# Attention mix on one core: width of the V products, queues of the Q and K moves, and the planner's numbers around them

## The chip, the cores and the metric

The kernel runs on one core of a Trainium2 chip. The metric is the device time of one execution in microseconds; each kernel is timed in several runs and the median counts. Engines are named as in the profile: PE (TensorE matmul) with PEld (its weight loads), ACT (ScalarE), DVE (VectorE), POOL (GpSimd) and SP (SyncE). SP and POOL matter here as queues too: each starts DMA transfers in the order of its own program, and a transfer that has to wait holds everything behind it on that queue.

## The reference

Two attention layers read the same input `x` (2048 rows of 512) and are mixed by a gate per row. Layer A has 32 heads of 16 columns that share one K and one V; layer B has a K and a V for each head.

```
g = sigmoid((x * gate_w).sum(-1, keepdims=True))
# A: q = x @ wq (32 heads of 16), k = x @ wk (16), v = x @ wv (16)
# B: q, k, v = x @ wqkv (32 heads of 16 each)
p = softmax(q @ k.T * 16 ** -0.5)      # per head, 2048 x 2048
o = p @ v
a = o_heads_joined @ wo
return g * a + (1 - g) * b
```

There are 64 heads in all, so 64 x 2048 x 2048 exponentials. Scores and probabilities stay on the core.

## The kernel before, in words

The heads are worked in 8 groups of eight (A and B in turn), each group for two halves of the query rows, each half for two sets of four heads: 32 phases. A phase has 32 *quads*, and a quad is two score tiles of 128x1024. So there are 2048 score tiles. Each is made by 8 matmuls of 512 columns on PE (names `sc`, line L564), which run side by side on tiles of 64x32 of the array, into one of two PSUM buffers. ACT takes the exponential of the tile into a buffer `prob` (L571). Some of the tiles go another way: PE writes them into the spare PSUM buffer, and DVE works out the exponential as a chain of 7 operations, one conversion (L751), two masks (L754, L758) and four steps of a polynomial (L763), into buffers `vec`. Both kinds are then multiplied with V on PE (L612) and summed in PSUM.

PSUM has two further buffers, `pair[0]` and `pair[1]`. One sums the V products of the phase; the other, the *spare*, is used by everything else in turn: projections of Q, K and V (24 products of 512 columns each, L188, from `project`), the turning of V (`turned`), the output projections (`o_unit`), and the score tiles for DVE. Each of these fills the spare on PE, and DVE then has to empty it before the next may begin. DVE and PE each work strictly in the order of their program.

A projection of Q or K is emptied by DVE as a high and a low fp16 part, `hi` and `lo` (L394, L397), and `lay` then moves 16-row pieces of them into the layout that the scores read: 32 DMAs for each projection. All of them are issued by POOL (L352). When a phase's sums are complete, DVE copies them to `raw` (L665), SP issues 10 moves of them into `dT` (the sums of the probabilities) and `oT` (L505, from `normalised`), and DVE takes the reciprocal (L511) and multiplies. Weights come one after another (`load_w`): SP loads one, POOL splits it into a high and a low half (L204 to L206), SP makes a copy with the partition halves swapped (`swapped`, L193), and DVE takes an absolute maximum of it (L197) for a check of the input's range.

The order of all this isn't written out by hand. The program is generated by a planner (`_Plan`, `pe_step`) that carries a clock of its own for each engine, charges each job a fixed price, and gives PE the next job that fits. `limit` is the time by which the next score tile has to begin: the later of the time at which it can (`t`) and `SLACK` ns behind the start of the last exponential. `value_job` offers a V product in pieces, 256 columns for tiles from ACT and 128 columns for tiles from DVE, where 256 columns are priced at `HALF` = 430 ns. `spare_job` decides between a projection and a tile for DVE: if no unit is in a hurry (its due time less than `SPARE` ns away), it is a tile for DVE. `ISSUE` is the price of a move, `LANDS` the time until it has landed. If a price is wrong, the order stays as it was planned, and an engine waits.

## Time and profile before

| | |
|---|---|
| Median of 3 runs | 2022.6 us (2015.66 to 2030.31) |
| Profiled execution, its own time | 2003.99 us |
| Its span | 2001.7 us |
| Mean granted clock of PE | 0.98 |
| ACT busy | 1816.2 us, 91% of the span |
| PE busy | 1840.3 us, 92% |
| DVE busy | 1198.4 us, 60% |
| POOL busy | 542.4 us, 27% |
| Exponentials on ACT / score tiles on DVE | 1946 / 102 |

The profile is of one execution. Busy time of a PE that pipelines its matmuls isn't a measure of its peak, so the table alone doesn't tell which engine sets the time; for that, one looks at what the idle time of each engine waits for. A row of the timeline gives start and length in us, engine, line, operation, and in brackets the idle time just before and what ended it. A row of the waits gives the total in us, how often, and the longest.

### The profile page before, as it was taken

What the parts mean: (1) busy time and instruction counts of PE and PEld (TensorE: products, weight loads), DVE (VectorE), ACT (ScalarE), POOL (GpSimd) and SP (SyncE); (2) the same over time, 40 slices, a digit from 0 to 9 for tenths busy, and PEclk for the clock granted to TensorE, in tenths of its full rate; (3) what the DMA queues carried; (4) which work ended last, traced back from release to release, by engine and by line L of the source; (5) the groups of instructions that cost most, each with busy time, mean ns of one, the idle gap of its engine ahead of it and who ended that gap; (6) DMA issues with size and microseconds to landing.
All of it is one profiled execution on the core that took longest, in us unless ns stands there. A gap on an engine that the chain in (4) does not pass through costs nothing.

```text
span 2001.7 us, 130978 instructions
## 1 busy us (share of the span) xinstructions
PE 1840.3 (92%) x61680; PEld 1155.0 (58%) x61680; DVE 1198.4 (60%) x1352; ACT 1816.2 (91%) x1961; POOL 542.4 (27%) x891
## 2 busy tenths in 40 slices
PE   8999998998999998998999999899799999898995
PEld 5566564555565665655666566555466565555552
DVE  5166521968385734578457752687657775158983
ACT  4899996998999998998999999899799999998994
POOL 4314303451042503325013430353203233034000
PEclk9999999999999999999999999999999999999997
DMA  5222212223132232133224241141402314116011
GB/s 140 47 34 47 68 36 72 46 56 62 30 62 44 50 56 51 37 62 66 47 40 79 43 70 20 40 87 42 76 5 49 64 38 76 32 27 162 15 57 56
DMA packets 140435, 109.73 MB, mean 55 GB/s; under 512 B 86432, under 2 KB 94880, under 8 KB 139888
## 3 DMA queue, kind: packets, MB, share of 16 engines
q0 software_dynamic: 37376, 50.35, 14.6%
q1 hardware_dynamic: 100560, 48.27, 10.2%
q8 instruction: 485, 7.95, 1.6%
q10 hardware_dynamic: 1952, 2.66, 0.4%
q14 instruction: 62, 0.51, 0.1%
HBM read 14.75 MB, written 33.55 MB: 24 GB/s over the span
## 4 chain that ended last, share of the span: by engine, by line
PE 47%; ACT 31%; issue 9%; DVE 6%; POOL 4%; DMA 2%; SPq 1%; ACTq 0%; DVEq 0%; POOLq 0%
ACT prob L571 31%; PE pair L612 23%; PE sc L564 13%; PE pair L188 8%; DVE vec L763 2%; POOL Qa L352 2%; DVE sum L471 1%; DVE vec L751 1%; SPq L505 1%; PE pair L564 1%; POOL K L352 1%; PE pt L265 1%; DMA wqb<-in_B_wqkv_dram 1%; DVE raw L665 0%; DMA oT<-raw 0%
## 5 line engine op out<-in xcount | busy, mean ns | idle before, releaser
L571 ACT ACTIVATE prob<-sc 128x1024 f32<-128x1024 f32 x1946 | 1805.6, 1093 | 128.3 <-PE sc L564 124.4
L612 PE MATMUL pair<-prob,vA 64*32 64x256 f32 x15680 | 695.8, 378 | 16.9 <-issue 15.7
L612 PE MATMUL pair<-prob,vB 64*32 64x256 f32 x15456 | 657.7, 381 | 11.6 <-issue 10.6
L564 PE MATMUL sc<-Qa,kA 64*32 64x512 f16 x7840 | 477.9, 383 | 18.3 <-issue 6.3
L564 PE MATMUL sc<-Qb,K 64*32 64x512 f16 x7728 | 442.6, 388 | 25.7 <-issue 4.2
L612 PEld LDWEIGHTS pair<-prob,vA 64*32 64x32 f32 x15680 | 350.3, 105 | 81.2 <-issue 38.8
L763 DVE SCALAR_TENSOR_TENSOR vec<-vec,vec 128x1024 f32<-128x1024 f32 x306 | 373.3, 1236 | 2.4
L564 PEld LDWEIGHTS <-K 64*32 64x32 f16 x8192 | 209.0, 91 | 282.5 <-issue 210.9
L612 PEld LDWEIGHTS pair<-prob,vB 64*32 64x32 f32 x15456 | 329.5, 106 | 71.4 <-issue 29.2
L564 PEld LDWEIGHTS <-kA 64*32 64x32 f16 x8192 | 213.3, 90 | 212.2 <-issue 157.1
L352 POOL DMA_DIRECT2D K<-hikb x128 | 65.7, 518 | 385.3 <-DVE hikb L394 382.7
L751 DVE TENSOR_SCALAR vec<-pair 128x1024 int32<-128x1024 f32 x102 | 124.1, 1217 | 71.9 <-PE pair L564 71.2
L352 POOL DMA_DIRECT2D Qa<-hiqa x115 | 59.6, 518 | 360.6 <-DVE hiqa L394 348.8
L763 DVE SCALAR_TENSOR_TENSOR vec<-vec 128x1024 f32<-128x1024 f32 x102 | 125.1, 1226 | 1.0
L481 POOL DMA_DIRECT2D out_dram<-sum x48 | 59.7, 1243 | 239.2 <-DVE sum L471 215.3
L511 DVE RECIPROCAL dT<-dT 128x256 f32<-128x256 f32 (+1 forms) x66 | 111.0, 1690 | 18.8 <-DMA dT<-raw 18.8
L352 POOL DMA_DIRECT2D Qb<-hiqb x128 | 66.2, 517 | 200.1 <-DVE hiqb L394 197.8
L471 DVE TENSOR_SCALAR sum<-pair,gate_up 128x512 f32<-128x512 f32 x112 | 78.5, 740 | 50.9 <-PE pair L188 50.7
L665 DVE COPY raw<-pair 128x1024 f32<-128x1024 f32 x32 | 39.1, 1222 | 116.7 <-PE pair L612 116.5
L188 PE MATMUL pair<-w16ob,o 64*32 64x512 f16 x1536 | 92.1, 396 | 15.3 <-ACT o L517 7.0
L188 PE MATMUL pair<-xT,w16kb 64*32 64x512 f16 x1536 | 101.6, 376 | 4.7 <-issue 4.6
L188 PEld LDWEIGHTS <-o 64*32 64x32 f16 x3072 | 60.7, 94 | 64.4 <-issue 27.4
(137 smaller groups left out, 1564.1 us busy)
## 6 DMA issues: line engine op xcount, KB each, us to landing
out_dram<-sum POOLq DMA_DIRECT2D x48, 512.0 KB, 5.9
dT<-raw SPq DMA_DIRECT2D x126, 64.0 KB, 2.7
vB<-vB SPq DMA_DIRECT2D x32, 128.0 KB, 5.1
Qb<-hiqb POOLq DMA_DIRECT2D x128, 32.0 KB, 2.3
Qb<-loqb POOLq DMA_DIRECT2D x128, 32.0 KB, 2.2
K<-hikb POOLq DMA_DIRECT2D x128, 32.0 KB, 2.3
K<-lokb POOLq DMA_DIRECT2D x128, 32.0 KB, 2.3
out_dram<-sum SPq DMA_DIRECT2D x8, 512.0 KB, 4.3
```

Of the source, the lines that this page charges most:

```text
L188: nc.tensor.matmul(outs[n : n + COLS, i], lhs[i][rows(i), n : n + COLS], rhs[i][rows(i)], start=start, stop=stop)
L265: nc.tensor.matmul(pt[rows(i), 2 * c + w, :], x_tiles[k][:, i, at : at + ROWS], ident, start=c % 2 == w == 0, stop=c % 2 == w == 1)
L352: fns.append(lambda q=queues[(8 * p + n) % len(queues)], dst=dst, src=hilo[part][at]: q.dma_start(dst, src))
L471: nc.vector.tensor_scalar(state["sum"][:, e], pair[1][:, e], g, None, op0=ALU.mult)
L481: plan.on_pool([lambda: nc.gpsimd.dma_start(dst, state["sum"], accum_op=ALU.add)], t, 1500)
L511: nc.vector.reciprocal(d[:, c : c + cut], d[:, c : c + cut])
L564: nc.tensor.matmul(bank[a : a + COLS, hh], k[rows(hh), key : key + COLS], Q[src, gi, half, p][rows(hh), j * BLK : (j + 1) * BLK], start=Tr ...
L571: nc.scalar.activation(probs[u], sc, AF.Exp, scale=SCALE / (UP * UP))
L612: nc.tensor.matmul(pair[0][32 * k : 32 * k + 32, i, cols], v[rows(i)], probs[2 * m + k // 2][rows(i), hh, cols], start=first, stop=last)
L665: nc.vector.tensor_copy(state["raw"], full)
L751: nc.vector.tensor_scalar(tile("p").bitcast(I32), pair[1], SCALE / (UP * UP) / math.log(2) * 2.0 ** 23, None, op0=ALU.mult)
L763: nc.vector.scalar_tensor_tensor(p, m if i == 3 else p, VEC[i], m if i else w, op0=ALU.add, op1=ALU.mult)
```

## The change

V products are offered in one piece of 512 columns where the planner's room up to `limit` is at least 860 ns and the product hasn't been begun, else in pieces of 256, for tiles of both kinds. `SLACK` is 404 instead of 400. The moves of Q and K alternate between SP and POOL, with a clock for SP in the planner. The swapped copies of the weights are issued by POOL instead of SP. V's swapped copy is one transfer for each partition half instead of two. The rest are numbers and conditions of the planner: the price of a turn, the times of the buffers `sum`, a lower `SPARE`, 3000 ns of margin before a tile of the next phase is given to DVE, a bound `LATE` on jobs between the two tiles of a quad, and 30000 instead of 15000 ns for the reading of the output before the last group.

```diff
-SLACK = 400
+SLACK = 404
 TO_VEC, FROM_VEC, CHAINED = 255, 150, 130
-ISSUE, LANDS = 520, 3200
+ISSUE, ISSUE_SP, LANDS, SUM_LANDS = 480, 600, 3200, 6500
...
+    def on_sp(self, fns, ready, ns):
+
+        for fn in fns:
+            fn()
+            self.sp = max(self.sp, ready) + ns
+        return self.sp
...
         def halve():
             split_weight(pair[0][:, 0], pair[0][:, 1], w)
-            swapped(pair[1], pair[0], nc.sync)
+            swapped(pair[1], pair[0], nc.gpsimd)
...
-            at = plan.on_pool([halve], t, 3300)
+            at = plan.on_pool([halve], t, 4800)
...
         def put(hilo, t):
-            queue = (nc.gpsimd,)
             to = q_tiles(src, gi, half) if part == "q" else k_tiles(gi, half)
             parts = (0, 1, 0, 1) if part == "q" else (0, 0, 1, 1)
             for p in range(4):
-                done = plan.on_pool(lay(hilo, to[p], p, parts, queue), t, ISSUE)
+                fns = lay(hilo, to[p], p, parts, (nc.sync, nc.gpsimd))
+                done = max(plan.on_sp(fns[0::2], t, ISSUE_SP), plan.on_pool(fns[1::2], t, ISSUE))
                 ready[part, src, gi, half, p] = done + LANDS
...
-                swapped(vB[1][:, ts, :, 0], vB[0][:, ts, :, 0], nc.sync)
-                swapped(vB[1][:, ts, :, 2], vB[0][:, ts, :, 2], nc.sync)
+                done = plan.on_sp([lambda: swapped(vB[1][:, ts], vB[0][:, ts], nc.sync)], end, 2 * ISSUE_SP)
                 free["spare"] = end + FROM_VEC
                 free["hilo"] = end
-                ready["v", gi, half] = end + LANDS + 1000
+                ready["v", gi, half] = done + LANDS + 1000
...
-        jobs = [(lambda t=t, part=part: job(t, part), 155) for t in range(8) for part in range(2)]
+        jobs = [(lambda t=t, part=part: job(t, part), 60) for t in range(8) for part in range(2)]
...
-                    plan.on_pool([lambda: nc.gpsimd.dma_start(dst, state["sum"], accum_op=ALU.add)], t, 1500)
+                    done = plan.on_pool([lambda: nc.gpsimd.dma_start(dst, state["sum"], accum_op=ALU.add)], t, 1300)
+                sum_free[state["turn"]] = done + SUM_LANDS
...
+            begin = end + TO_VEC
+            if n + 1 < len(groups):
+                state["turn"] = turn[0]
+                turn[0] ^= 1
+                begin = max(begin, sum_free[state["turn"]])
             for e in range(2):
-                plan.vec(lambda e=e: take(e), 620, 1, end + TO_VEC, (), then if e else None)
+                plan.vec(lambda e=e: take(e), 660, 1, begin, (), then if e else None)
...
+        plan.sp = max(plan.sp, now) + len(moves) * ISSUE_SP
...
-    def value_job(now, mine):
+    def value_job(now, mine, room):
...
-        wide = BLK // (2 if mine else 4)
+        wide = BLK if n == 0 and room >= 2 * HALF else BLK // 2
         ns = HALF * wide * 2 // BLK
 
         def job():
-            values(m, slice(n * wide, (n + 1) * wide))
-            going[mine] = m, n + 1
-            if (n + 1) * wide == BLK:
+            values(m, slice(n, n + wide))
+            going[mine] = m, n + wide
+            if n + wide == BLK:
...
-            if max(laid(ph, NT - 1, phases[ph][2] + e) for e in range(2)) > now:
+            if max(laid(ph, NT - 1, phases[ph][2] + e) for e in range(2)) + 3000 > now:
...
-    JOB, AFTER, SPARE, WORK, EXTRA = 900, 3000, 20000, 1500, 7000
+    JOB, AFTER, SPARE, WORK, EXTRA, LATE = 900, 3000, 10000, 1500, 7000, 400
...
-        mine, other = (lambda: value_job(now, True)), (lambda: value_job(now, False))
+        mine, other = (lambda: value_job(now, True, limit - now)), (lambda: value_job(now, False, limit - now))
...
-            if job and now + job[1] <= limit:
+            if job and now + job[1] <= (limit if get is mine or not part[0] else min(limit, t + LATE)):
...
-        ready["late"] = plan.pe + 15000
+        ready["late"] = plan.pe + 30000
```

Since the planner sets the order, the change moves instructions all through the program. Counted over the whole order, ACT has 1926 exponentials instead of 1946 and DVE 122 tiles instead of 102. PE's V products (L612, now L624) stand in 12,624 matmuls instead of 17,200: 15,568 of 256 columns and 1,632 of 128 before, 3,760 of 512 and 8,864 of 256 now. Lines of the changed kernel are 7 to 12 higher. Three places follow.

The first is on PE, in the middle of the first group of layer A, where the second half of the keys of layer B's first group is projected (`w16kb00` is that weight; `pair` is a PSUM buffer; `sc276` is score tile 276). Before:

```order
L564 LDWEIGHTS K00_5601
L564 MATMUL sc276_7749<-Qb000_4410,K00_5601 32x512
L612 MATMUL pair1_83<-prob0_97,vB0_91 32x256 x4
L612 MATMUL pair1_83<-prob1_98,vB0_91 32x256 x4
L188 LDWEIGHTS w16kb00_737
L188 MATMUL pair0_82<-xT_84,w16kb00_737 32x512
```

Now the same projection begins here:

```order
L576 LDWEIGHTS kA_88
L576 MATMUL sc229_6473<-Qa013_2027,kA_88 32x512
L624 MATMUL pair0_82<-prob0_97,vA1_90 32x256 x4
L624 MATMUL pair0_82<-prob1_98,vA1_90 32x256 x4
L195 LDWEIGHTS w16kb00_737
L195 MATMUL pair1_83<-xT_84,w16kb00_737 32x512
```

The projection has moved from behind score tile 276 to behind score tile 229. Tile 288 is the first that reads this second half of the keys.

The second place is SP's queue, where the weights of the second group of layer B are loaded (`wkb1`, `wvb1`, `wqb1`; `w16...` are their halves; `raw5` and `oT102` belong to the normalisation of phase 5). Before:

```order
L505 DMA oT102_10671<-raw5_10669 32x512
L505 DMA oT102_10671<-raw5_10669 16x512
L193 DMA w16kb11_10574<-w16kb10_10573 64x1024 x2
L219 DMA wvb1_10843<-in_B_wqkv_dram 128x4x128
L193 DMA w16vb11_10846<-w16vb10_10845 64x1024 x2
L219 DMA wqb1_11011<-in_B_wqkv_dram 128x4x128
L193 DMA w16qb11_11014<-w16qb10_11013 64x1024 x2
```

Now:

```order
L516 DMA oT102_9975<-raw5_9973 32x512
L516 DMA oT102_9975<-raw5_9973 16x512
L359 DMA Qa100_10038<-hiqa10_10008 16x1024 x4
L359 DMA Qa101_10039<-hiqa10_10008 16x1024 x4
L359 DMA Qa102_10040<-hiqa10_10008 16x1024 x4
L359 DMA Qa103_10041<-hiqa10_10008 16x1024 x4
L226 DMA wvb1_10116<-in_B_wqkv_dram 128x4x128
L226 DMA wqb1_10241<-in_B_wqkv_dram 128x4x128
```

The copies of the halves have gone from this queue, and half of the moves of a Q projection stand ahead of the two loads.

The third place is DVE at the same time of the program (`stats` are the maxima, `sum0` takes an output projection out of the spare buffer, `vec` belongs to the chains). Before:

```order
L197 TENSOR_REDUCE stats_87<-w16kb10_10573 128x1
L763 SCALAR_TENSOR_TENSOR vec1_104<-vec1_104,vec5_108 128x1024
L197 TENSOR_REDUCE stats_87<-w16vb10_10845 128x1
L763 SCALAR_TENSOR_TENSOR vec1_104<-vec1_104,vec6_109 128x1024
L197 TENSOR_REDUCE stats_87<-w16qb10_11013 128x1
L471 TENSOR_SCALAR sum0_110<-pair1_83,gate_up_96 128x512 x2
```

Now:

```order
L204 TENSOR_REDUCE stats_87<-w16kb10_9877 128x1
L775 SCALAR_TENSOR_TENSOR vec6_109<-vec0_103 128x1024
L204 TENSOR_REDUCE stats_87<-w16vb10_10118 128x1
L476 TENSOR_SCALAR sum0_110<-pair0_82,gate_up_96 128x512 x2
L775 SCALAR_TENSOR_TENSOR vec6_109<-vec6_109,vec0_103 128x1024
L204 TENSOR_REDUCE stats_87<-w16qb10_10243 128x1
L775 SCALAR_TENSOR_TENSOR vec6_109<-vec6_109,vec0_103 128x1024
```

The emptying of the spare into `sum0` now stands ahead of the maximum of `w16qb`, and one operation of a chain lies between the maxima of `w16kb` and `w16vb` as before.

11 lines of the change are left out of this document (5 added, 6 removed).

## The prediction, made before the changed kernel was run

> **What bounds the kernel now.** I read the page first, then ACT's timeline, then what PE waited for, then each large gap on the engines around it.
>
> ```profile
> span 2001.7 us, 130978 instructions
> PE 1840.3 (92%) x61680; PEld 1155.0 (58%) x61680; DVE 1198.4 (60%) x1352; ACT 1816.2 (91%) x1961; POOL 542.4 (27%) x891
> PE 47%; ACT 31%; issue 9%; DVE 6%; POOL 4%; DMA 2%; SPq 1%; ACTq 0%; DVEq 0%; POOLq 0%
> L571 ACT ACTIVATE prob<-sc 128x1024 f32<-128x1024 f32 x1946 | 1805.6, 1093 | 128.3 <-PE sc L564 124.4
> ```
>
> PE and ACT look equally full, and the chain runs through both. ACT's timeline decides; these are a run without a gap and the gaps that the sum below uses:
>
> ```profile
> 176.74 81.81 ACT L571 ACTIVATE prob<-sc 128x1024 f32<-128x1024 f32 x89 [0.66 <-PE sc L564]
> ...
> 321.54 1.02 ACT L571 ACTIVATE prob<-sc 128x1024 f32<-128x1024 f32 x1 [14.86 <-PE sc L564]
> 324.99 65.30 ACT L571 ACTIVATE prob<-sc 128x1024 f32<-128x1024 f32 x71 [2.42 <-PE sc L564]
> ...
> 448.68 1.02 ACT L571 ACTIVATE prob<-sc 128x1024 f32<-128x1024 f32 x1 [2.19 <-PE sc L564]
> ...
> 457.64 1.03 ACT L571 ACTIVATE prob<-sc 128x1024 f32<-128x1024 f32 x1 [3.65 <-PE sc L564]
> ...
> 940.90 1.02 ACT L571 ACTIVATE prob<-sc 128x1024 f32<-128x1024 f32 x1 [4.51 <-PE sc L564]
> ...
> 1416.43 1.02 ACT L571 ACTIVATE prob<-sc 128x1024 f32<-128x1024 f32 x1 [8.47 <-PE sc L564]
> ```
>
> 89 exponentials in 81.81 us, the last one 1.02 long: (81.81 - 1.02) / 88 = 0.918 us each. 1946 of them make 1786 us, and the waits for PE 124.4; together 1911 of 2001.7, the rest being start, end and the last exponential of each run. So **ACT is the bound**, and PE costs time only where it is late with a score tile. Why it is late:
>
> ```profile
> PE pair L612 <- issue: 31.9, 44, 2.9
> PE pair L564 <- DVE sum L471: 15.8, 3, 8.2
> PE pair L564 <- DMA K<-lokb: 12.6, 8, 3.2
> PE sc L564 <- issue: 10.5, 17, 2.0
> ...
> PE pair L188 <- issue: 5.2, 6, 2.6
> PE pair L420 <- issue: 4.0, 7, 0.8
> ```
>
> **The change part by part.** *Fewer exponentials on ACT.* The order has 1926 instead of 1946: 20 x 0.918 = **-18.4 us**. They become chains on DVE:
>
> ```profile
> L763 DVE SCALAR_TENSOR_TENSOR vec<-vec,vec 128x1024 f32<-128x1024 f32 x306 | 373.3, 1236 | 2.4
> L751 DVE TENSOR_SCALAR vec<-pair 128x1024 int32<-128x1024 f32 x102 | 124.1, 1217 | 71.9 <-PE pair L564 71.2
> ```
>
> Four steps of 1.24, one conversion of 1.22 and two masks, taken at most as long as that: at most 7 x 1.24 = 8.7 us a chain, 174 us for 20. DVE goes from 60% to at most 69%, beside the exponentials; what its cover costs where it is gone is in the costs below.
>
> *The second half of layer B's first keys.* The gap of 14.86 us is in the plan itself:
>
> ```profile
> 307.61 2.43 PE L188 MATMUL pair<-xT,w16kb 64*32 64x512 f16 x72
> 312.62 2.76 PE L188 MATMUL pair<-w16oa,o 64*32 64x512 f16 x48 [2.58 <-DVE lokb L397]
> ```
> ```profile
> 311.60 0.96 POOL L352 DMA_DIRECT2D K<-hikb  x2 [78.84 <-DVE hikb L394]
> ...
> 326.79 0.49 POOL L352 DMA_DIRECT2D K<-lokb  x1
> ```
>
> The last products of the projection run at 307.61 to 310, with no score among them, POOL issues the moves from 311.60 to past 327, and tile 288 can't start before its first eight have landed. In the new order the projection begins 59 tiles ahead of tile 288 instead of 12, which is 47 x 0.918 = 43 us more, against a gap of 17. Both gaps go: 14.86 + 2.42 = **-17.3**. Nothing stands ready to take their place: no other stretch between two scores in the new order holds over 1.3 us of PE work, once the start is over.
>
> *K tiles that hadn't landed.* The waits for `K<-lokb` are 12.6 us in 8 pieces: tiles of the next phase given to DVE too early. They go from two sides: 32 moves at 0.48 on one queue (15.4 us) become 16 on each, and the planner adds 3 us of margin. I take **-11**, between 0 and -12.6.
>
> *Maxima that wait for weights.* At 446 to 457 this is what held PE:
>
> ```profile
> 446.82 1.10 SPq L193 DMA_DIRECT2D w16vb<-w16vb  x2
> 448.02 0.54 SPq L219 DMA_DIRECT2D wqb<-in_B_wqkv_dram  x1
> ```
> ```profile
> 452.12 1.49 POOL L204 TENSOR_SCALAR wqb<-wqb 128x512 f32<-128x512 f32 x1 [5.33 <-DMA wqb<-in_B_wqkv_dram]
> ```
> ```profile
> 454.33 0.69 DVE L197 TENSOR_REDUCE stats<-w16qb 128x1 f32<-128x512 f16 x1 [6.46 <-POOL w16qb L205]
> ```
> ```profile
> 456.38 0.73 PE L564 MATMUL pair<-Qb,K 64*32 64x512 f16 x8 [3.11 <-DVE sum L471]
> ```
>
> The load of `wqb` stands on SP behind the copy of `w16vb`, which waits for POOL; so POOL waits for the load, DVE's maximum for POOL, the emptying of the spare stands behind that maximum, and PE behind the spare. This happens in three of the four groups, with gaps on ACT of 2.19 + 3.65, 4.51 and 8.47: 18.8 us. With the copies on POOL's queue both loads are under way together, and POOL's next split finds its weight there. In place of that stand 16 moves ahead of the loads, at the most 16 x 0.59 = 9.4 us (SP's issue of such a move, in a row below), while POOL has its own 16 moves of 0.48 and the split of `wkb` to do. I take **-15**, between 0 and -18.8. The copies cost POOL two issues a weight, some 1 us, in an engine that is busy 27% and loses 368 moves.
>
> *Fewer instructions on PE.* "Issue" in PE's waits is time for which the profile shows no cause: 31.9 + 10.5 + 5.2 + 4.0 = 51.6 us. One of them, with the rows of the page that bear on it:
>
> ```profile
> 480.36 0.41 PE L564 MATMUL sc<-Qb,K 64*32 64x512 f16 x7
> 482.76 0.37 PE L564 MATMUL sc<-Qb,K 64*32 64x512 f16 x1 [2.00 <-issue]
> ```
> ```profile
> q8 instruction: 485, 7.95, 1.6%
> ...
> out_dram<-sum POOLq DMA_DIRECT2D x48, 512.0 KB, 5.9
> ```
>
> PE stops within the 8 matmuls of one tile, whose inputs are the same. 7.95 MB over 2 x 61680 instructions is 64 bytes each, so this queue feeds PE, 16 KB (256 instructions) every 4.1 us. My reading: a refill is held up by a big transfer, such as the 512 KB additions that take 5.9 us to land. Each V matmul of the order is two matmuls and two loads in the profile (7840 against 15680), so 4,576 fewer make 18,304 fewer of 123,360, or 15%, and what PE has in stock lasts 17% longer: 1.0 us over a hold-up of 5.9. The pauses have a mean of 51.6 / 74 = 0.7 us, so most could vanish. Bounds 0 and -51.6; I take **-25**, half, since not all need come from this.
>
> [...]
>
> *Pieces of 512 columns* stream as long as two of 256, but keep a score waiting for 0.86 us instead of 0.43. The trace has such a stretch:
>
> ```profile
> 104.79 0.41 PE L564 MATMUL sc<-Qa,kA 64*32 64x512 f16 x8 [0.51 <-ACT prob L571]
> 105.01 1.06 PE L612 MATMUL pair<-prob,vA 64*32 64x256 f32 x32
> 105.87 0.41 PE L564 MATMUL sc<-Qa,kA 64*32 64x512 f16 x8
> ```
>
> Scores 1.08 us apart, against 0.918. The new order has 581 stretches of this length between scores, before 18. If nothing covered them, 581 x 0.16 = 93 us; but two score buffers let PE be early by up to a tile, and 283 stretches with at most one product in them stand between. Bounds 0 and +93; I take **+5**, nearest to the cover.
>
> *SP's queue* gets 368 moves more. Its issue of one (shortest, median and longest, in ns), its moves after one phase, and what they waited for:
>
> ```profile
> L352 SPq DMA_DIRECT2D Qa<-hiqa x11: 507/587/1549, 22.0 to 32.0; - x11
> ```
> ```profile
> 412.99 2.94 SPq L505 DMA_DIRECT2D dT<-raw  x4
> 415.97 4.22 SPq L505 DMA_DIRECT2D oT<-raw  x6
> ...
> SPq L505 <- DVE raw L665: 1106.2, 30, 56.2
> ```
>
> SP was idle for `raw` 30 times, so the moves of `dT` went at once. Where 16 moves of 0.59 stand directly ahead, `dT` comes up to 9.4 us later, and DVE's reciprocal is planned 6.5 us behind `raw`. In the order that is so at one place, phase 4 (the K moves above, now ahead of its `raw`). **+5** for this, **+5** for the fuller DVE, from bounds of 0 and 9.4 each.
>
> V's copy in one transfer, the prices of a turn and of the additions, and the 30 us before the last group's reading are off the path: no row has PE waiting for `vB`, and behind that reading three more normalisations stand in SP's order, phases of up to 64 exponentials of 0.918 us, against 15 us of delay. I take 0.
>
> **The sum**: -18.4 - 17.3 - 11 - 15 - 25 + 15 = -72. Against the profiled execution (span 2001.7, its time 2003.99) that is 1932. The three runs had a median of 2022.6, 0.9% above it, so I take the gain from that: **1951 us**.
>
> **The rivals.** *Pauses stay.* If they come from something that doesn't count instructions, 25 us are missing: 1976. For it: I infer the cause. [...]
>
> *The stalls move.* Planned places change, but prices remain estimates; if the K and weight waits turn up elsewhere at the old size, 26 are missing: 1977.
>
> *Long pieces delay scores.* At half the price above, 47 - 5 more: 1993; at the full price, 2039. It decides where PE has no tile in hand. Against it: the plan lets a score begin 404 ns behind an exponential, before 400.
>
> *SP's queue becomes the bound*, the case that ends slower. If moves of Q and K stand ahead of `dT` at many of the 31 normalisations, DVE waits up to 9.4 us in each and PE for the spare, as in the gap of 8.47. It cancels the gain of 87 from about ten places on; at twelve, 12 x 9 = 108 instead of 5: 2054. Against it: the one place in the order.
>
> That the change doesn't do what it says is excluded by the counts of the order.
>
> **How the numbers follow.** Forecast 0.46 (its own range 1925 to 1975), better, with all pauses gone, 0.10 (1924), pauses stay 0.18, stalls move 0.06, long pieces 0.10, SP 0.10. Measurement can tell about 1% from no change, 2002 to 2043. The first four are faster: 0.80; of the long pieces 0.04 faster, 0.04 same, 0.02 slower; of SP 0.03 same, 0.07 slower. That makes 0.84, 0.07 and 0.09. The range reaches down to 1905, where the waits and pauses go whole and the costs are nothing (18.4 + 17.3 + 12.6 + 18.8 + 51.6 = 119), and up to 2005, past the pieces at half price; it leaves out the slow ends, about 0.15.
>
> **What would show it.** ACT has 1926 exponentials and no gap above 5 us between tiles 230 and 330; waits of PE for `K<-lokb` and for `sum` fall to a few us; "issue" of PE falls to about 25. Wrong if the mean distance of exponentials in a run without gaps rises above 0.93 (long pieces), if DVE waits for `dT<-raw` for over 50 us (SP, 15.8 before), or if new gaps of over 60 us in sum stand behind the spare.

## The result, and the profile after

The changed kernel takes **1920.7 us** (median of 4 runs, 1918.33 to 1922.41) against 2026.45 us before (median of 4, one run more than before the prediction). The ratio is **0.948**, with a 95% interval of 0.944 to 0.953. The profiled execution took 1918.33 us, and its span fell by 85.1 us, from 2001.7 to 1916.6. By the medians the gain is 105.7 us. The difference of some 20 us belongs mostly to the kernel before: its profiled execution (2003.99) was faster than all four of its timed runs (2015.66 to 2032.98), while the changed kernel's runs agree within 4 us. Ratios leave out executions of the kernel before that lie over 1.5% above its fastest (four of the twelve timed beside width_alone, queues_alone, spare_alone and onequeue below), so there a ratio isn't quite that of the medians.

The first view is the page of the changed kernel: the span, the busy time of the engines, the instruction queue of PE, the chain of work that ended last, and the group of the exponentials.

```profile
span 1916.6 us, 112936 instructions
PE 1759.1 (92%) x52528; PEld 1000.5 (52%) x52528; DVE 1341.1 (70%) x1492; ACT 1792.8 (94%) x1941; POOL 385.3 (20%) x569
q8 instruction: 413, 6.77, 1.5%
ACT 57%; PE 24%; issue 13%; DVE 2%; DMA 2%; POOL 1%; SPq 1%; ACTq 0%; DVEq 0%; POOLq 0%
L583 ACT ACTIVATE prob<-sc 128x1024 f32<-128x1024 f32 x1926 | 1782.2, 1072 | 65.5 <-PE sc L576 61.2
```

The last row accounts for the span. ACT's exponentials took 23.4 us less (1805.6 to 1782.2), and ACT's idle time before them fell by 62.8 us (128.3 to 65.5), together 86.2, against the 85.1 by which the span fell. PE's row says the same from the other side: its busy time fell by 81.2 us and its idle time hardly at all (161.4 to 157.5). The chain, which ran through PE for 47% of the span and through ACT for 31%, now runs through ACT for 57%.

ACT's timeline after: a run without a gap, the stretch in which the gap of 14.86 us stood before, and the three largest gaps that are left in the middle of the kernel.

```profile
131.87 118.81 ACT L583 ACTIVATE prob<-sc 128x1024 f32<-128x1024 f32 x129 [1.55 <-PE sc L576]
251.66 1.94 ACT L583 ACTIVATE prob<-sc 128x1024 f32<-128x1024 f32 x2 [0.98 <-PE sc L576]
255.07 3.77 ACT L583 ACTIVATE prob<-sc 128x1024 f32<-128x1024 f32 x4 [1.46 <-PE sc L576]
260.24 22.86 ACT L583 ACTIVATE prob<-sc 128x1024 f32<-128x1024 f32 x24 [1.40 <-PE sc L576]
284.36 2.10 ACT L583 ACTIVATE prob<-sc 128x1024 f32<-128x1024 f32 x2 [1.26 <-PE sc L576]
...
442.55 1.02 ACT L583 ACTIVATE prob<-sc 128x1024 f32<-128x1024 f32 x1 [5.66 <-PE sc L576]
...
894.34 1.02 ACT L583 ACTIVATE prob<-sc 128x1024 f32<-128x1024 f32 x1 [3.37 <-PE sc L576]
...
1357.39 1.02 ACT L583 ACTIVATE prob<-sc 128x1024 f32<-128x1024 f32 x1 [4.81 <-PE sc L576]
```

The pace without a gap is (118.81 - 1.02) / 128 = 0.920 us, against 0.918 before. The gap of 14.86 us has become four of at most 1.46. The gaps at the weights of a new group are still there. What PE waited for:

```profile
PE sc L576 <- ACT prob L583: 60.5, 171, 0.5
PE pair L624 <- issue: 12.3, 18, 1.7
PE sc L576 <- issue: 9.0, 12, 1.6
PE pair L576 <- DVE sum L476: 8.7, 4, 4.5
...
PE pair L427 <- issue: 4.9, 4, 1.3
PE pair L195 <- issue: 3.8, 6, 1.4
...
PE pair L576 <- DMA K<-lokb: 1.7, 3, 1.2
PE pair L576 <- issue: 0.9, 2, 0.6
```

The row of the kernel before that belongs to the first of these:

```profile
PE sc L564 <- ACT prob L571: 4.6, 10, 1.0
```

PE now waits 171 times instead of 10 for ACT to free a score buffer: it is ahead of ACT where it was late before. "Issue" has fallen from 51.6 to 30.9 us, and the waits for K tiles from 12.6 to 1.7.

### The profile page after: what moved, and what is told of

The parts are those of the page before. It is cut to its first block, busy times and chain, and to the rows that moved or that the text cites. A ratio compares the mean times of both kernels' runs of the same rounds, so it can differ in the third digit from the quotient of the medians.

```text
span 1916.6 us, 112936 instructions
## 1 busy us (share of the span) xinstructions
PE 1759.1 (92%) x52528; PEld 1000.5 (52%) x52528; DVE 1341.1 (70%) x1492; ACT 1792.8 (94%) x1941; POOL 385.3 (20%) x569
## 3 DMA queue, kind: packets, MB, share of 16 engines
q0 software_dynamic: 27808, 44.30, 13.8%
## 4 chain that ended last, share of the span: by engine, by line
ACT 57%; PE 24%; issue 13%; DVE 2%; DMA 2%; POOL 1%; SPq 1%; ACTq 0%; DVEq 0%; POOLq 0%
ACT prob L583 57%; PE pair L624 11%; PE sc L576 6%; PE pair L195 5%; SPq L359 1%; DMA wvb<-in_B_wqkv_dram 1%; PE pt L272 1%; DMA wqb<-in_B_wqkv_dram 1%; PE pair L576 1%; POOL wvb L211 1%; PE pair L427 1%; DVE sum L476 0%; DVE vec L763 0%; PE pair L272 0%; DVE xT L470 0%
## 5 line engine op out<-in xcount | busy, mean ns | idle before, releaser
L583 ACT ACTIVATE prob<-sc 128x1024 f32<-128x1024 f32 x1926 | 1782.2, 1072 | 65.5 <-PE sc L576 61.2
L624 PE MATMUL pair<-prob,vA 64*32 64x256 f32 (+1 forms) x12368 | 607.8, 433 | 8.4 <-issue 7.7
L624 PE MATMUL pair<-prob,vB 64*32 64x256 f32 (+1 forms) x10928 | 561.0, 461 | 4.2 <-issue 3.7
L576 PE MATMUL sc<-Qa,kA 64*32 64x512 f16 x7824 | 440.3, 380 | 28.2 <-ACT prob L583 16.9
L576 PE MATMUL sc<-Qb,K 64*32 64x512 f16 x7584 | 410.9, 382 | 56.4 <-ACT prob L583 44.6
L775 DVE SCALAR_TENSOR_TENSOR vec<-vec,vec 128x1024 f32<-128x1024 f32 x366 | 448.5, 1236 | 3.3
L624 PEld LDWEIGHTS pair<-prob,vA 64*32 64x32 f32 x12368 | 260.9, 106 | 55.5 <-issue 16.0
L624 PEld LDWEIGHTS pair<-prob,vB 64*32 64x32 f32 x10928 | 219.5, 106 | 45.2 <-issue 11.6
L359 POOL DMA_DIRECT2D Qa<-loqa x122 | 61.5, 513 | 387.4 <-DVE loqa L404 167.3
L523 DVE RECIPROCAL dT<-dT 128x256 f32<-128x256 f32 (+1 forms) x66 | 110.8, 1690 | 22.6 <-DMA dT<-raw 22.6
L359 POOL DMA_DIRECT2D Qb<-loqb x128 | 64.8, 514 | 278.5 <-PE sc L576 277.2
L766 DVE TENSOR_SCALAR vec<-vec 128x1024 int32<-128x1024 int32 x122 | 84.9, 696 | 1.8
L770 DVE TENSOR_SCALAR vec<-vec 128x1024 int32<-128x1024 int32 x122 | 86.1, 706 | 0.0
```

The lines of the kernel that those rows point to most:

```text
L359: fns.append(lambda q=queues[(8 * p + n) % len(queues)], dst=dst, src=hilo[part][at]: q.dma_start(dst, src))
L523: nc.vector.reciprocal(d[:, c : c + cut], d[:, c : c + cut])
L576: nc.tensor.matmul(bank[a : a + COLS, hh], k[rows(hh), key : key + COLS], Q[src, gi, half, p][rows(hh), j * BLK : (j + 1) * BLK], start=Tr ...
L583: nc.scalar.activation(probs[u], sc, AF.Exp, scale=SCALE / (UP * UP))
L624: nc.tensor.matmul(pair[0][32 * k : 32 * k + 32, i, cols], v[rows(i)], probs[2 * m + k // 2][rows(i), hh, cols], start=first, stop=last)
L766: nc.vector.tensor_scalar(tile("m").bitcast(I32), tiles["p"].bitcast(I32), 0x7FFFFF, 125 << 23, op0=ALU.bitwise_and, op1=ALU.bitwise_or)
```

## The experiments

The columns below: the median; the ratio to the kernel before, timed beside it; and from the profiled execution all of PE's "issue" rows together (53.5 us for the kernel before and 32.6 for the changed one, counting 1.9 and 1.7 us of a row at the start that is left out above), PE's busy time, and ACT's idle time before exponentials. The last four kernels ran on a second chip, on which the kernel before had a median of 2016.06 (2009.06 to 2020.16; on the first chip 2002.62 to 2044.37), so they are compared with the others by their ratios.

| kernel | us | ratio, 95% interval | "issue" | PE busy | ACT idle |
|---|---|---|---|---|---|
| before | 2026.45 | 1 | 53.5 | 1840.3 | 128.3 |
| changed | 1920.7 | 0.948, 0.944 to 0.953 | 32.6 | 1759.1 | 65.5 |
| width_alone | 1939.97 | 0.962, 0.955 to 0.969 | 16.2 | 1762.8 | 87.8 |
| queues_alone | 2037.98 | 1.011, 1.003 to 1.018 | 62.5 | 1847.8 | 155.9 |
| spare_alone | 2023.2 | 1.002, 0.998 to 1.006 | 78.2 | 1853.8 | 161.1 |
| onequeue | 1922.85 | 0.952, 0.945 to 0.960 | 26.9 | 1758.0 | 69.5 |
| swapsp | 1925.45 | 0.948, 0.943 to 0.953 | 27.7 | 1759.9 | 69.5 |
| inp2 | 1906.11 | 0.938, 0.933 to 0.943 | 30.7 | 1758.7 | 56.7 |
| split512 | 1968.56 | 0.970, 0.963 to 0.976 | 48.1 | 1789.2 | 103.5 |
| noadd | 1983.96 | 0.977, 0.971 to 0.984 | 38.6 | 1839.9 | 109.3 |
| all256 (second chip) | 1963.62 | 0.972, 0.968 to 0.976 | 47.7 | 1785.6 | 101.2 |
| after_noadd (second chip) | 1884.9 | 0.936, 0.933 to 0.938 | 12.3 | 1740.3 | 28.8 |
| split_noadd (second chip) | 1922.0 | 0.955, 0.951 to 0.958 | 25.3 | 1765.0 | 64.8 |
| adds4 (second chip) | 1883.39 | 0.934, 0.931 to 0.937 | 17.0 | 1747.0 | 36.1 |

### Which part of the change carries the gain

Three parts, each done alone on the kernel before. First the widths:

```diff
-SLACK = 400
+SLACK = 404
...
-        wide = BLK // (2 if mine else 4)
+        wide = BLK if n == 0 and room >= 2 * HALF else BLK // 2
...
```

> The kernel before with one part of the change: the widths of the V products (512 where it fits, else 256) with the slack of 404. The order holds 18 exponentials fewer on ACT and as few matmuls as the changed kernel (within 0.2%). By the forecast's terms: 18 x 0.918 = 16.5 us, 'issue' from 51.6 to some 31 (21 us), pieces of 512 at +5: some 33 us less, between 15 and 45. If the count of instructions doesn't matter, 16.5 us less and 'issue' above 45.

Measured: 86.5 us less, far more than the 15 to 45 expected, and 82% of the whole gain (74% by the ratios). ACT's exponentials and what PE waited for in this kernel:

```profile
L571 ACT ACTIVATE prob<-sc 128x1024 f32<-128x1024 f32 x1928 | 1782.4, 1073 | 87.8 <-PE sc L564 84.8
```
```profile
PE pair L564 <- DVE sum L471: 29.2, 7, 8.2
...
PE pair L612 <- issue: 6.5, 11, 1.6
...
PE pair L564 <- DMA K<-lokb: 4.6, 3, 3.0
```

On ACT, the exponentials took 23.2 us less and the idle time before them 40.5 us less, together 63.7 of the 64.1 us by which this span (1937.6) is below that of before. On PE, "issue" fell by 37.3 us. This order also shortens the gap of 14.86 us; its largest there is 2.54.

Then the moves on two queues:

```diff
-ISSUE, LANDS = 520, 3200
+ISSUE, ISSUE_SP, LANDS = 480, 600, 3200
...
-                done = plan.on_pool(lay(hilo, to[p], p, parts, queue), t, ISSUE)
+                fns = lay(hilo, to[p], p, parts, (nc.sync, nc.gpsimd))
+                done = max(plan.on_sp(fns[0::2], t, ISSUE_SP), plan.on_pool(fns[1::2], t, ISSUE))
...
```

> The kernel before with one part of the change: the moves of Q and K alternate between SP and POOL, and the planner keeps a clock for SP. The order holds 2 exponentials fewer on ACT and as many matmuls. By the forecast's terms: the waits for K tiles go (-11 us), 2 x 0.92 for the exponentials, and nothing of PE's 51.6 us of 'issue': 1 to 14 us less than before. If the big gain comes from the many small moves that no longer stand on one queue (and not from the count of instructions), 'issue' falls below 40 us here and the time by 25 or more. By the rival in which SP becomes the bound, DVE's waits for transposed outputs rise over 50 us and the time rises.

Measured: 1% slower (0.3 to 1.8%), and the waits that it was to remove have grown from 12.6 to 30.5 us:

```profile
PE pair L572 <- DMA K<-lokb: 30.5, 10, 7.8
```

A likely reason: the planner now counts K as laid sooner and gives tiles of the next phase to DVE earlier than the moves land. In the whole change it waits 3000 ns more before such a tile, which this kernel doesn't. The reverse, the order of the changed kernel with all moves on POOL:

```diff
-                fns = lay(hilo, to[p], p, parts, (nc.sync, nc.gpsimd))
+                fns = lay(hilo, to[p], p, parts, (nc.gpsimd,))
```

> The changed kernel, in its own order, with all moves of Q and K issued by POOL. A group of 32 moves at 0.48 us takes 15.4 us on one queue instead of 7.7 on each of two, while the order was planned for two. If the two queues carry the gain of the K tiles, the waits for moved K tiles return (1.7 to 15 us or more) and new gaps stand before the first tiles of phases: 10 to 40 us above the changed kernel. If the moves have room either way (the planner now lays them earlier), the time is within 5 us of 1921.

Measured: 1922.85, the same as the changed kernel. One wait has grown, from 1.7 to 6.1 us, and with it a gap has come back on ACT, where PE waits 4.98 us for a move of layer B's first keys:

```profile
PE pair L576 <- DMA K<-lokb: 6.1, 3, 5.0
```
```profile
286.80 1.02 ACT L583 ACTIVATE prob<-sc 128x1024 f32<-128x1024 f32 x1 [6.11 <-PE sc L576]
```

The time doesn't show it; another gap is smaller in this execution (1.62 us ended at 431.95, where the changed kernel has 5.66 ended at 442.55). So the second queue accounts for 4.4 of the 10.9 us by which the waits for K fell, and the order for the rest. The margin of 3000 ns is a candidate, which wasn't tried alone; the widths alone, without it, already leave only 4.6 of the 12.6 us.

Third, the reserve that decides when spare work is begun:

```diff
-    JOB, AFTER, SPARE, WORK, EXTRA = 900, 3000, 20000, 1500, 7000
+    JOB, AFTER, SPARE, WORK, EXTRA = 900, 3000, 10000, 1500, 7000
```

> The kernel before with one number of the planner changed, the reserve that decides when spare work is begun (20000 to 10000). The order holds 4 exponentials fewer on ACT. If this number alone set the late projection of layer B's first keys, the gaps of 14.86 and 2.42 us before tiles 288 go: 4 x 0.918 + 17.3 = 21 us less. If that came from the planner's clocks for the queues or from the widths, the gaps stay and the time is within 6 us of the kernel before.

Measured: no change (0.998 to 1.006). The two gaps are there as before, 7 us later, so this number isn't what moved the projection:

```profile
328.88 1.02 ACT L571 ACTIVATE prob<-sc 128x1024 f32<-128x1024 f32 x1 [14.87 <-PE sc L564]
332.67 2.85 ACT L571 ACTIVATE prob<-sc 128x1024 f32<-128x1024 f32 x3 [2.77 <-PE sc L564]
```

### The weights of a new group

> The changed kernel with the swapped copies of the weights issued by SP again, in the same order. The forecast put the shorter waits for maxima down to the copies' move to POOL's queue. If that is so, the three gaps on ACT (13.8 us together) grow back to some 18.8 and the time by 5 us; if the copies also stand ahead of the moves of Q and K on SP, the waits for K tiles come back as well (1.7 to some 10 us), 10 to 14 us in all. Rival: the copies' queue does nothing, because the load behind them waits for the buffer that POOL's split gives back either way: within 3 us of 1921.

```diff
-            swapped(pair[1], pair[0], nc.gpsimd)
+            swapped(pair[1], pair[0], nc.sync)
```

Measured: 1925.45 against 1920.7, with ratios that agree (0.948), so the time alone doesn't decide. The three gaps on ACT do; they have grown from 13.8 to 19.1 us:

```profile
442.80 1.03 ACT L583 ACTIVATE prob<-sc 128x1024 f32<-128x1024 f32 x1 [6.33 <-PE sc L576]
...
895.74 1.02 ACT L583 ACTIVATE prob<-sc 128x1024 f32<-128x1024 f32 x1 [6.00 <-PE sc L576]
...
1358.20 1.02 ACT L583 ACTIVATE prob<-sc 128x1024 f32<-128x1024 f32 x1 [6.77 <-PE sc L576]
```

That is the first expectation: the copies' queue is worth some 5 us of the gaps, not the 15 of the prediction. These rows of the changed kernel, of SP, POOL, DVE and PE at one of the three gaps, say why:

```profile
878.04 0.53 SPq L226 DMA_DIRECT2D wvb<-in_B_wqkv_dram  x1
885.75 0.37 SPq L226 DMA_DIRECT2D wqb<-in_B_wqkv_dram  x1
```
```profile
884.55 1.17 POOL L213 TENSOR_TENSOR w16vb<-wvb,w16vb 128x512 f16<-128x512 f32 x1
...
889.26 1.48 POOL L211 TENSOR_SCALAR wqb<-wqb 128x512 f32<-128x512 f32 x1 [2.13 <-DMA wqb<-in_B_wqkv_dram]
```
```profile
891.45 0.69 DVE L204 TENSOR_REDUCE stats<-w16qb 128x1 f32<-128x512 f16 x1 [5.12 <-POOL w16qb L212]
```
```profile
893.51 0.51 PE L576 MATMUL pair<-Qb,K 64*32 64x512 f16 x8 [3.76 <-DVE sum L476]
```

The load of `wqb` goes out at 885.75, directly behind the end of POOL's split of `wvb` (884.55 + 1.17 = 885.72). All weights are loaded into one buffer of the pool `inp`, so the next load can't begin before POOL has done with the one before, whichever queue the copies are on. With two such buffers:

```diff
-    inp = ctx.enter_context(tc.tile_pool(name="inp", bufs=1))
+    inp = ctx.enter_context(tc.tile_pool(name="inp", bufs=2))
```

> The changed kernel with two buffers instead of one for the weights as they are loaded. Theory: the term of the maxima came out small (5 of 18.8 us) because the load of a group's next weights waits until POOL has split the ones before and given back the only buffer. With two, the load of wqb is issued without that wait, POOL finds it landed, and ACT's three gaps of 5.66, 3.37 and 4.81 us at 442, 894 and 1357 go: 10 to 14 us less, near 1909. Rival: POOL itself is late (its split takes up to 7.5 us beside DVE and its moves stand ahead), then SP's wait goes but DVE's wait for POOL stays near 21.5 us and the time within 4 us of 1921.

The same place in that kernel:

```profile
873.52 0.53 SPq L226 DMA_DIRECT2D wvb<-in_B_wqkv_dram  x1
874.15 0.52 SPq L226 DMA_DIRECT2D wqb<-in_B_wqkv_dram  x1
```
```profile
883.11 1.48 POOL L211 TENSOR_SCALAR wqb<-wqb 128x512 f32<-128x512 f32 x1
```
```profile
885.30 0.69 DVE L204 TENSOR_REDUCE stats<-w16qb 128x1 f32<-128x512 f16 x1 [3.07 <-POOL w16qb L212]
```

Both loads are out together, POOL finds `wqb` there, and the maximum comes 6 us earlier. DVE's waits for `w16qb` fall from 21.5 to 6.8 us. The time is 1906.11, 14.6 us below the changed kernel by the medians and just past the upper end of what the theory gave; the profiled execution, the slowest of its four, is 7.1 us below. The rival, that POOL itself is late, falls.

### What the pieces of 512 columns do

The changed kernel with each such piece issued as two of 256 at the same place in the order:

```diff
-            values(m, slice(n, n + wide))
+            for c in range(n, n + wide, BLK // 2):
+                values(m, slice(c, c + BLK // 2))
```

> The changed kernel, each V product of 512 columns issued as two of 256 at the same place in the order; everything else is the same. 470 pieces are split, so PE executes some 60,050 matmuls and as many loads (52,528 each in the changed kernel, 61,680 before). If PE's pauses without a shown cause hang on how many instructions PE runs, they go from 30.9 us back to 45 to 52, and the time is 15 to 21 us above the changed kernel's 1921, near 1940. If they hang on something else (the big transfers, the fewer moves), PE's 'issue' stays within 5 us of 30.9 and the time within 5 us of 1921. A third way: the pieces of 512 held up scores; then the split kernel is faster, by up to 19 us.

```profile
PE 1789.2 (91%) x60048; PEld 1152.6 (59%) x60048; DVE 1337.7 (68%) x1492; ACT 1802.7 (92%) x1941; POOL 383.6 (20%) x569
L583 ACT ACTIVATE prob<-sc 128x1024 f32<-128x1024 f32 x1926 | 1792.1, 1061 | 103.5 <-PE sc L576 97.6
```
```profile
PE pair L624 <- issue: 25.2, 30, 1.8
...
PE sc L576 <- issue: 9.1, 16, 1.6
```

Measured: 47.9 us above the changed kernel, where 15 to 21 were expected. "Issue" came back as the theory said (32.6 to 48.1, or 15.5 us), but PE's busy time rose by 30.1 us too, and ACT's idle time by 38.0. The third way, that long pieces hold up scores, falls: with the long pieces the kernel is faster.

Is it the matmuls themselves? Where the step from one block of 256 instructions to the next (it is counted below) doesn't fall inside, a piece of 512 takes 857 ns from its first matmul to the start of what follows (median of 379 in the changed kernel), and two of 256 in a row take 861 (median of 326 here). For 470 pieces that is 2 us, and by the means (863 and 878 ns) 7 us, not 48. Planned for 256 throughout, with as many matmuls as here, the kernel comes out in the same place:

```diff
-        wide = BLK if n == 0 and room >= 2 * HALF else BLK // 2
+        wide = BLK // 2
```

> The changed kernel planned with V products of 256 columns throughout: as many matmuls as with each 512 split in two (45,200 of the order), 1926 exponentials on ACT as well, but the planner may put a score between two pieces. If a piece costs PE the same wherever it stands, the time is that of the split kernel, 1969 within 8 us. If it is two pieces in a row that cost (a score held up behind both, or the second one's loads not hidden), it lies clearly below, near 1935 to 1950; the rest of the way to the kernel before's 2026 then comes from its pieces of 128 and its 20 exponentials.

Measured: a ratio of 0.972 against 0.970 for the split kernel, so two pieces in a row aren't the matter either. It is the number of instructions. The next count shows where they cost time. All instructions of PE in the trace (weight loads, matmuls and some 250 others, mostly waits of its sequencer) are numbered from 0 in the order of their start, and the distances of over 1 us between two starts are counted, with how many of them (and how much time) stand within the same 8 positions out of every 256. By chance it would be 1 in 32. The last column is all the time, short distances included, between the instructions at positions 192 and 193; a usual position has about 7 us.

```
kernel        over 1 us   of them at the same position of 256   us in these   all at 192
before            53          25                                   43.6          110.2
spare_alone       74          43                                   71.6          152.1
noadd             46          16                                   20.5          102.8
width_alone       37          14                                   25.7           49.5
changed           40          24                                   35.1           65.1
inp2              39          24                                   35.1           63.8
split512          46          31                                   49.4          102.1
all256            48          32                                   49.2          104.5
after_noadd       27          11                                   15.2           29.7
split_noadd       33          16                                   24.6           62.2
adds4             26          11                                   16.2           42.7
```

It is behind position 192 in every one of these kernels, and nearly always to the instruction: all 25 of the kernel before stand there. So does every pause that the profile names "issue": 75 of 75 before, 43 of 43 in the changed kernel. The instruction queue has 485 packets of 16,384 bytes before and 413 in the changed kernel, for 123,608 and 105,276 instructions of PE: one packet for 255 of them, or 64 bytes each. So these pauses of PE stand where one block of instructions ends and the next hasn't come. The prediction inferred this; here it is shown. The packets of that queue in the trace agree: in each of the 25 and 24 long pauses there, PE goes on 1.2 to 1.6 us after such a packet has ended, and at no step of these two kernels sooner than 1.18 us.

The split adds 37.0 us at this position (65.1 to 102.1), of the 48.1 us by which the span grows. More than half of it isn't in the rows of the waits: "issue" shows 15.5. The granted clock is a second, smaller cost: before the last 30 us, the changed kernel has 13.7 us in which PE runs at half its clock and the split one 27.3, which is at most 6.8 us more of lost work.

Why 14% more instructions cost so much can be read from the same packets. In the kernel before a refill starts 1.1 us (median) behind the previous step from block to block, its packet takes 1.0 us, and PE went on no sooner than 1.2 us later: 3.3 us, of the 4.1 in which this PE uses up a block on average. The changed kernel takes 4.7 us for a block. Ahead of the pauses of over 1 us the refill starts later, at a median of 2.5 us before and 3.0 in the changed kernel, while its packet takes no longer. The refill is late because it begins late.

Most of these steps have no pause: 152 of 482 have one of over 0.15 us in the kernel before, 83 of 410 in the changed one. These few hold 103.1 of the 110.2 us of the table, and 60.7 of the 65.1.

### What holds up the refills

The kernel before and the changed one without the 48 additions of 512 KB to the output:

```diff
-                    plan.on_pool([lambda: nc.gpsimd.dma_start(dst, state["sum"], accum_op=ALU.add)], t, 1500)
+                    plan.on_pool([lambda: None], t, 1500)
```

> The kernel before without the 48 additions of 512 KB to the output on POOL's queue: what the middle groups of heads add to the output is left out, the order of everything else is the same. The reading in the prediction was that a refill of PE's instructions is held up by such a transfer. If so, PE's 'issue' falls from 51.6 us to under 15 and the time by 30 to 40 us. If the refills are late by themselves (the number of instructions alone), PE's 'issue' stays within 8 us of 51.6 and the time within 8 us of the kernel before.

Measured: 46 us less than before by the medians (16.9 between the profiled executions), but "issue" only from 53.5 to 38.6, and all the time at position 192 only from 110.2 to 102.8. Its longest pause in a row of V products is 1.7 us instead of 2.9; there are as many of them:

```profile
PE pair L612 <- issue: 22.0, 47, 1.7
```

In the kernel before, the additions lengthen some of the pauses; they aren't their only cause. So neither of the two expectations holds alone.

> The changed kernel without the 48 additions of 512 KB to the output (what the middle groups of heads add to the output is left out). Without them the kernel before lost 46 us by its medians, and PE's 'issue' 15 us by its profiles, mostly in shorter pauses. If the additions cost time because they hold up the refills of PE's instructions, the changed kernel, which has 15% fewer of these, loses less: 'issue' from 30.9 to some 20 us, the time by 8 to 20 us to 1900-1913. If they cost time in another way (the load on the memory, waits for sums), the loss is as large as before, 35 to 50 us.

Measured: the ratio falls from 0.948 to 0.936, which is 1.3% or 26 us (36 us by the medians of the two chips), and "issue" from 32.6 to 12.3. That is more than the 8 to 20 us expected: the changed kernel, with 15% fewer instructions, still lost much to the additions. Of the 44.0 us by which the span falls, 35.4 lie at position 192, and the refill ahead of a long pause now starts 1.1 us (median) behind the step before instead of 3.0.

> The kernel with each piece of 512 split at the same place, and without the 48 additions (again that part of the output is left out). The split alone cost 48 us, of which PE's 'issue' shows some 15 and PE's busy time 30. Theory of two costs: the pauses at refills shrink without the additions, but the 32 us for two pieces where one would do stay, so this kernel is 30 to 40 us above the changed kernel without additions. If the whole cost of the split were refills held up by the additions, it is less than 15 us above it.

Measured: 37.1 us above the changed kernel without additions, timed beside it, with 13.0 us more of "issue" and 24.7 more of PE's busy time. Most of what a split costs is there without the additions too. The number was expected, but not for this reason: the theory held it for a cost of the matmuls themselves, and 32.5 of the 46.1 us between the two spans lie at position 192. More instructions cost time there even without the additions. This is PE's row in the kernel without additions, and then in the split one:

```profile
PE 1740.3 (93%) x52528; PEld 993.5 (53%) x52528; DVE 1334.5 (71%) x1492; ACT 1786.3 (95%) x1941; POOL 322.0 (17%) x521
```
```profile
PE 1765.0 (92%) x60048; PEld 1140.4 (59%) x60048; DVE 1334.3 (70%) x1492; ACT 1795.4 (94%) x1941; POOL 324.0 (17%) x521
```

At last the changed kernel with two buffers for weights, and each addition issued as four of 128 columns. The bytes are the same; a row of an addition is 512 bytes instead of 2 KB:

```diff
-                    done = plan.on_pool([lambda: nc.gpsimd.dma_start(dst, state["sum"], accum_op=ALU.add)], t, 1300)
+                    done = plan.on_pool([lambda c=c: nc.gpsimd.dma_start(dst[:, :, c : c + 128], state["sum"][:, :, c : c + 128], accum_op=ALU.add) for c in range(0, 512, 128)], t, 325)
```

> The changed kernel with two buffers for weights, and each addition to the output issued as four of 128 columns (512 bytes a row in place of 2 KB). If a refill of PE's instructions is held up by long packets that stand ahead of it, shorter ones let it through: PE's 'issue' falls from 27 us to under 20, and the time from 1906 to some 1898. If it waits for the queues' total work, nothing changes, or the four times as many packets make the additions land later and the waits for sums cost 0 to 15 us: 1906 to 1920.

```profile
PE 1747.0 (93%) x52528; PEld 1003.7 (53%) x52528; DVE 1342.8 (71%) x1492; ACT 1789.9 (95%) x1941; POOL 562.6 (30%) x713
out_dram<-sum POOLq DMA_DIRECT2D x192, 128.0 KB, 4.6
```
```profile
PE pair L624 <- issue: 4.9, 9, 0.9
PE sc L576 <- issue: 3.3, 7, 1.4
```

Measured: **1883.39 us, a ratio of 0.934** (0.931 to 0.937), the fastest of all kernels here with the whole output, and clearly below the changed kernel's 0.948. Against two buffers alone (0.938, on the other chip) the step is 0.4% by the ratios and 22.7 us by the medians, so its size isn't settled; but "issue" falls from 30.7 to 17.0 and the time at position 192 from 63.8 to 42.7, as the theory of long packets said, with the same instructions on PE and the same bytes. Each addition also became four smaller transfers, issued one after another; whether the shorter rows or the smaller transfers did it wasn't separated. POOL pays for it with 185 us more of busy time (378.0 to 562.6) and has them to spare.

## Why the prediction was right, and where it was wrong

The forecast was 1951 us, faster by about 4%; the result is 30 us below it, inside the range. Step by step:

- *Fewer exponentials on ACT* (-18.4). Right: the group has 1926 of them and 23.4 us less of busy time. DVE is at 70%, where at most 69 was given.
- *The second half of layer B's first keys* (-17.3). Right in mechanism: no gap of over 1.46 us is left there. The four gaps before the exponentials at 251 to 284 sum to 5.1 us, so some 12 were gained. It came by the order together with the second queue: the reserve alone didn't do it, and with one queue a gap of 6.11 us is back there.
- *K tiles that hadn't landed* (-11). The size is right (12.6 to 1.7), its working only in part. "32 moves at 0.48 on one queue become 16 on each" explains 4.4 us, since back on one queue the waits are 6.1; the two queues alone, in the order that the planner then makes, even lengthened the waits to 30.5. The rest is the new order, to which the widths alone bring most (4.6 left); what the margin adds wasn't tried.
- *Maxima that wait for weights* (-15). This step failed: 18.8 us became 5.66 + 3.37 + 4.81 = 13.8. "With the copies on POOL's queue both loads are under way together" is false, because there was one buffer for both loads; with a second one it becomes true, and 14.6 us go. The copies' queue itself gave the 5 us: with the copies back on SP the gaps are 19.1. The chain of waits was read rightly down to SP, but the load behind the copy had two things to wait for, and only the later one shows.
- *Fewer instructions on PE* (-25). Right in mechanism, and the rows named "issue" gave nearly the forecast, 20.7 us. The term was sized from these rows alone, and that is too small: all the time at the step from block to block fell by 45.1 us (110.2 to 65.1), and in the same order the split of the long pieces brings 37.0 us of it back, of which the rows of "issue" show 15.5. The stock that the prediction set against a hold-up of 5.9 us looks like one block, 4.1 us of PE's work before and 4.7 now: all refills but 1 of 482 and 2 of 410 started behind the step before. The rival that the pauses stay falls.
- *Pieces of 512 columns* (+5). No cost to be seen: the pace without a gap is 0.920 us. The rival of delayed scores falls.
- *SP's queue* and *the fuller DVE* (+5 each). DVE waited 22.6 us for `dT`, before 18.8; no new gap stands behind the spare. The rival of SP's queue as the bound falls.

The sum was -72 against the profiled execution, whose span fell by 85.1; that it came so near is partly luck, since the shortfall of the first keys and of the maxima (5 and 10 us) was made up by 15 us of costs that didn't come. Of the miss of 30 us, 13 are the sum's. The other 17 come from a choice, "I take the gain from that", that is, from the median: it took the gain to be the same for every run. The kernel before loses more in its usual runs than in the one that was profiled. That this is at the steps from block to block is likely but not shown: the profiled runs of spare_alone, queues_alone and before took 2040.44, 2033.75 and 2003.99 us and have 152.1, 133.6 and 110.2 us at position 192, with nearly as many matmuls (61,744, 61,712 and 61,680), but the three have different orders. And "ACT is the bound" was half true: PE's busy time fell by nearly as much as the span, while ACT had been idle for 128 us before its exponentials.

Three things stay open. The widths alone have less "issue" (16.2 us) than the whole change (32.6), and less time at position 192 (49.5 against 65.1), with as many instructions, so the order or the shape of the other transfers matters as well; V's copy in one transfer of longer rows would be a candidate and wasn't tried alone. What delays the start of a refill when no addition is under way isn't known. And of the split's 48.1 us, the block steps and the clock account for at most 44; the rest is within what the pieces themselves may cost (2 to 7 us), but isn't shown.

## What to carry to other kernels

Where PE runs tens of thousands of small matmuls, its instruction supply can be a cost of its own, as it was here with 61,680 of them: number all its instructions by their start, and look whether the pauses stand at one position, here of every 256. If they do, add up all the time at that position, not only the named pauses: here it was 110.2 of 2001.7 us before; in the changed order the wide pieces save 37.0 us there, and splitting another engine's big transfers took off 21.1. Before the removal of a wait is counted, look for the second thing that the same instruction waits for, here a buffer.

## What the runs showed of the hardware

In the changed kernel PE's granted clock fell to 0.72 and 0.73 at two of the gaps that are left on ACT. These stretches, which hold the gaps that ended at 442.55 and 894.34, give the stretch and its length, the busy time of PE, PEld, DVE, ACT and POOL (with the number of instructions), then the granted clock, the share of the DMA engines and their GB/s:

```profile
440.00:446.00 6.00, 5.06 (x128) 2.64 (x135) 4.45 (x5) 2.59 (x3) 1.44 (x2) 0.72 0.82 134
...
892.00:898.00 6.00, 4.49 (x77) 2.53 (x84) 5.22 (x8) 2.96 (x3) 3.10 (x4) 0.73 0.57 90
```

With two buffers for weights these gaps are gone, and so are these dips:

```profile
440.00:446.00 6.00, 5.89 (x192) 3.61 (x184) 5.00 (x7) 5.49 (x7) 1.14 (x1) 1.00 0.03 5
...
890.00:896.00 6.00, 4.58 (x151) 2.54 (x143) 6.00 (x7) 4.88 (x6) 0.00 (x0) 1.00 0.54 85
```

One gap of 3.04 us is left nearby, ended at 429.50, where PE waits for a chain of DVE, and there the clock is halved for 3.41 us from 429.31.

The gaps of 3.4 to 5.7 us went with a mean clock of 0.72 to 0.73 over the 6 us around their end, so such a stall can cost somewhat more than its own length. The trace has a stretch of 3.41 us at half clock at each of the three (from 440.82, 894.79 and 1355.59), which takes 0.28 of 6 us. PE had stood still there for 5.26, 3.76 and 4.48 us, but shorter stalls went with it too: the pause of 2.00 us that ends at 482.76 in the kernel before is followed by half clock from 483.01, while no such stretch stands at the one of 2.01 us that ends at 1331.24. In these two kernels PE was idle for 1.94 us or more of the 3.41 us ahead of every stretch at half clock.

The other new things are that in these two kernels PE began no block of instructions sooner than 1.18 us after a packet of its queue had ended, and that splitting the additions, transfers that have nothing to do with PE, into four with shorter rows shortened PE's pauses, from 30.7 to 17.0 us of "issue".
